# Second MoE, first product: product 6 joins products 1, 7 and 4 in one PSUM bank

## The chip, the cores and the metric

The kernel runs on one core of a Trainium2 chip. The metric is the device time of one execution in microseconds (us). The kernel before takes 1375.94 us, the median of 3 runs (1375.69 to 1376.54).

## The reference, cut to what matters

Three layers follow each other: pooled attention, a first MoE block with softplus, and a second MoE block with a router. The change lies in the first product of the second MoE block, `x @ w1[e]`, with the relu behind it:

```
def _moe2_ref(x, expert_emb, tau, w1, w2):
    N, D = x.shape                       # 4608, 512
    ...                                  # router: expert_idx, gate_w
    for e in range(E):
        mask = expert_idx == e
        h = np.maximum(x[mask] @ w1[e], 0.0)          # w1[e]: 512 x 1024
        out[mask] = gate_w[mask, None] * (h @ w2[e])
```

## The kernel before, in words

The second MoE block is computed for the expert that has most tokens over all 4608 tokens; other experts' tokens are left to a loop behind it, which has nothing to do in the run shown. The tokens come in 9 groups of 512 (`p` = 0 to 8), called pairs here, since each is two halves of 256 tokens. For every pair `mm3s(p, sg)` is called with `sg` 0 and 1, and each call makes two steps `j` of 128 hidden columns (with their partners 512 columns on). So there are 18 calls and 36 steps.

One step is a Strassen-like scheme with seven products in place of eight: two halves of `w1` rows, two of its columns, two halves of the tokens. A product (`prod`) is six matmuls of 128x128 by 128x256 into a PSUM bank: two chunks of 128 rows, and for each the three float32r products of high and low parts (`three`, lines 656 to 658). Products 1, 2 and 3 read the tokens (tile `b`), 4 to 7 read sums of them (tile `T`, made by `make_t` on GpSimd and `split_t` on ScalarE and VectorE). The results wanted are: 1+2 (hidden low, tokens low), 1+6+3+5 (low, high), 1+6+7+5 (high, high) and 1+6+7+4 (high, low). `put` makes two float32r parts of relu of such a result: ScalarE writes the high part (line 1025), VectorE the rest (line 1026).

TensorE's and SyncE's orders are those of the code. The orders of VectorE, ScalarE and GpSimd in this stage come from the framework's scheduler, so a new code order may reorder them. All engines work in order. `both` runs the two steps of a call, then three pieces of the second product (`mm4s`, nine matmuls of 128x512), then the last step's `end`, then the other 13 pieces. Where a bank is written again (`skip_group_check`), the first matmul of the product waits until the reading of the bank is done; with its weight load waits.

TensorE's order of products is, for the two steps of a call (the second with a prime): before 1, 6, 5, 2, 7, 1', 4, 3, 6', 5', 2', 7', three pieces, 4', 3'. The bank `b2` gathers products 6, 7 and 4, `b3` gathers 5 and 3, `b1` gathers 1 and 2. Four PSUM banks, with the tags `h` and `a` (two each), go round by the list `M_TAGS`.

Of the kernel before, what the change touches and what calls it, by code (L numbers as in the profile page):

```python
# [13 lines left out]
ALU = mybir.AluOpType  # L14
# [6 lines left out]
def tile_attention_moe_moe(  # L21
# [13 lines left out]
    nc = tc.nc  # L35
# [40 lines left out]
    def f32(ap):  # L76
        return ap.bitcast(F32)
# [5 lines left out]
    half = cp.tile([P, TPB], F32, name="half")  # L83
# [571 lines left out]
    def three(ps, lh, ll, rh, rl, first, last, more=False):  # L655
        nc.tensor.matmul(ps, ll, rh, start=first, stop=False, skip_group_check=more)  # L656
        nc.tensor.matmul(ps, lh, rl, start=False, stop=False, skip_group_check=more)  # L657
        nc.tensor.matmul(ps, lh, rh, start=False, stop=last, skip_group_check=more)  # L658
# [337 lines left out]
    def g_tile(k):  # L996
        pool = {"g": p2[0], "st": stp, "W": wp, "wo": wop}[HOMES[k]]
        kw = {"bufs": 3} if HOMES[k] == "g" else {}
        return pool.tile([P, 2, PT], F32R, tag=HOMES[k], name=f"g{k}", **kw)


    def mm3s(p, sg):
        x, t = b_t[p], t_t[p]
        direct = {1: 0, 2: 2, 3: 1}
        sums = {4: 1, 5: 0, 6: 2, 7: 3}

        def prod(bank, i, j, first):
            if i in direct:
                bh, bl = x[direct[i]][:, 0], x[direct[i]][:, 1]
            else:  # L1010
                bh, bl = t[:, 0, sums[i]], t[:, 1, sums[i]]
            ff = slice(j * P, (j + 1) * P)
            for c in range(2):
                w = a_t[i, c]
                three(bank, w[:, 0, ff], w[:, 1, ff], bh[:, c, :], bl[:, c, :], first and c == 0, c == 1, not first)

        def bank():
            tag = M_TAGS.pop(0)
            M_TAGS.append(tag)
            return (ps_h if tag == "h" else ps_a).tile([P, HT], F32, tag=tag, name="m")  # L1020


        def put(src, d, th):
            tt = slice(th * HT, (th + 1) * HT)
            nc.scalar.activation(d[:, 0, tt], src, AF.Relu)
            nc.vector.scalar_tensor_tensor(d[:, 1, tt], src, 0.0, f32(d)[:, 0, tt], ALU.max, ALU.subtract)

        def half(n):
            return p2[0].tile([P, HT], F32, tag=n, bufs=2, name=n)

        ends = []
        for j in (2 * sg, 2 * sg + 1):
            b1 = bank()
            prod(b1, 1, j, True)
            s1 = half("c1")
            nc.scalar.copy(s1, b1)
            if ends:
                ends.pop()()
            b2 = bank()
            prod(b2, 6, j, True)  # L1040
            s2 = half("c2")
            nc.vector.tensor_tensor(s2, b2, s1, ALU.add)
            b3 = bank()
            prod(b3, 5, j, True)
            prod(b1, 2, j, False)
            lo, hi = g_tile(2 * j), g_tile(2 * j + 1)
            gs_t[j], gs_t[j + 4] = lo, hi
            put(b1, lo, 0)
            prod(b2, 7, j, False)
            s3 = half("c3")  # L1050
            nc.vector.tensor_tensor(s3, b2, s1, ALU.add)
            nc.vector.tensor_tensor(s3, b3, s3, ALU.add)
            put(s3, hi, 1)

            def end(j=j, b2=b2, b3=b3, s1=s1, s2=s2, lo=lo, hi=hi):
                prod(b2, 4, j, False)
                nc.vector.tensor_tensor(s1, b2, s1, ALU.add)
                put(s1, hi, 0)
                prod(b3, 3, j, False)
                nc.vector.tensor_tensor(s2, b3, s2, ALU.add)  # L1060
                put(s2, lo, 1)

            ends.append(end)
        yield
        ends.pop()()

    M_TAGS = ["h", "h", "a", "a"]

    def mm4s(p, sg):
        if sg == 0 and p not in y_t:  # L1070
# [171 lines left out]
    with tc.block(schedule_with_timeline_sim=True), tc.manual_schedule(engines={mybir.EngineType.PE, mybir.EngineType.SP}):  # L1242
# [91 lines left out]

        load_b(1, (0, 1, 2))
        m3 = mm3s(0, 0)
        next(m3)
        run_mm2(*pend.pop(0))
# [3 lines left out]
        run(make_t(1))  # L1342
        fronts(WAIT + 1)
        both(mm3s(0, 1), mm4s(0, 0), WAIT2 + 3)
        for p in range(1, NPR):
            run(split_t(p))
            fronts(2)
            if p + 1 < NPR:
                load_b(p + 1)
                run(make_t(p + 1))  # L1350
            both(mm3s(p, 0), mm4s(p - 1, 1))
            fronts(1)
            both(mm3s(p, 1), mm4s(p, 0))
# [39 lines left out]
```

## Time and profile before

| | before |
|---|---|
| time, median of 3 runs | 1375.94 us |
| profiled execution: its own time | 1376.53 us |
| profiled execution: span of the trace | 1374.7 us |
| TensorE busy | 1350.0 us, 98% |
| VectorE busy | 763.5 us, 56% |
| ScalarE busy | 644.5 us, 47% |
| GpSimd busy | 281.4 us, 20% |
| share of TensorE in the chain that ended last | 83% |

The busy share of TensorE is near the whole span, so what matters in a stage is what TensorE waits for there. The second MoE block fills the stretch from about 974 us to the end.

### The profile page before, as it was taken

How to read it: one execution, taken by the hardware profiler on the slowest of the kernel's cores; microseconds unless marked ns; L12 is line 12 of the kernel's file. 1: busy time of each engine (PE TensorE's matmuls, PEld its weight loads, DVE VectorE, ACT ScalarE, POOL GpSimd, SP SyncE). 2: the span in 40 equal slices, each digit the busy share in tenths (PEclk: the TensorE clock that was granted, in tenths of full speed). 3: DMA queues.
4: the chain of work that ended last, by engine and by line, in shares of the span. 5: the costliest groups of instructions: out<-in, count | busy, mean ns of one | idle time of the engine just before them, and what ended most of it. 6: DMA issues, size and time to landing. Idle time of an engine off the chain costs nothing.

```text
span 1374.7 us, 18505 instructions
## 1 busy us (share of the span) xinstructions
PE 1350.0 (98%) x6998; PEld 1118.0 (81%) x6998; DVE 763.5 (56%) x1608; ACT 644.5 (47%) x1287; POOL 281.4 (20%) x268
## 2 busy tenths in 40 slices
PE   8999999999999999999999999999999999999998
PEld 7666678878888878888888888878878898998986
DVE  7997567566465466475564443353664544544432
ACT  5766455554465464564464454455532322222221
POOL 6500112121021020020020010073353022231100
PEclk9999999999999999999999999999999999999999
DMA  9742354353364363453442242563332212222000
GB/s 275 244 125 85 105 172 140 112 195 107 113 203 124 95 195 92 127 181 95 139 153 85 79 152 77 168 210 126 107 124 93 87 37 77 78 93 93 31 31 32
DMA packets 113564, 166.94 MB, mean 121 GB/s; under 512 B 42808, under 2 KB 69432, under 8 KB 113472
## 3 DMA queue, kind: packets, MB, share of 16 engines
q1 hardware_dynamic: 113472, 165.72, 38.2%
q8 instruction: 57, 0.93, 0.3%
q14 instruction: 35, 0.29, 0.1%
HBM read 128.99 MB, written 36.70 MB: 121 GB/s over the span
## 4 chain that ended last, share of the span: by engine, by line
PE 83%; DVE 8%; DMA 3%; POOL 2%; ACT 2%; issue 1%; SPq 1%; POOLq 0%; DVEq 0%; ACTq 0%
PE h L656 8%; PE h L658 8%; PE h L657 8%; PE acc L656 8%; PE acc L658 8%; PE acc L657 8%; PE y L656 5%; PE y L657 5%; PE y L658 5%; PE m L656 4%; PE m L658 4%; PE m L657 4%; PE pp L338 2%; PE acc L710 2%; PE lg L742 1%; DMA wos<-wo 1%
## 5 line engine op out<-in xcount | busy, mean ns | idle before, releaser
L656 PE MATMUL h<-x,wi 128*128 128x512 f32 x576 | 234.9, 408 | 1.2 <-DVE t L689 1.1
L658 PE MATMUL h<-x,wi 128*128 128x512 f32 x576 | 225.7, 392 | 0.0
L657 PE MATMUL h<-x,wi 128*128 128x512 f32 x576 | 225.0, 391 | 0.0
L672 ACT ACTIVATE t<-h 128x512 f32<-128x512 f32 x144 | 86.1, 598 | 229.5 <-PE h L658 222.7
L656 PE MATMUL acc<-g,ring 128*128 128x512 f32 x448 | 177.9, 397 | 0.1
L658 PE MATMUL acc<-g,ring 128*128 128x512 f32 x448 | 174.8, 390 | 0.0
L657 PE MATMUL acc<-g,ring 128*128 128x512 f32 x448 | 174.4, 389 | 0.0
L689 DVE SCALAR_TENSOR_TENSOR t<-h,t 128x512 f32<-128x512 f32 x128 | 87.9, 687 | 147.3 <-ACT t L676 146.1
L656 PEld LDWEIGHTS h<-x,wi 128*128 128x128 f32 x576 | 108.7, 189 | 24.4 <-DVE t L689 1.8
L658 PEld LDWEIGHTS h<-x,wi 128*128 128x128 f32 x576 | 108.4, 188 | 24.2
L657 PEld LDWEIGHTS h<-x,wi 128*128 128x128 f32 x576 | 108.8, 189 | 21.1 <-issue 1.0
L691 ACT CAST g<-t 128x512 fp32r<-128x512 f32 x128 | 79.6, 622 | 86.7 <-DVE t L689 86.6
L693 DVE TENSOR_TENSOR g<-t,g 128x512 fp32r<-128x512 f32 x128 | 92.0, 719 | 50.7 <-ACT g L691 50.6
L656 PE MATMUL y<-w,g 128*128 128x512 f32 x288 | 113.0, 392 | 0.0
L657 PE MATMUL y<-w,g 128*128 128x512 f32 x288 | 112.9, 392 | 0.0
L658 PE MATMUL y<-w,g 128*128 128x512 f32 x288 | 112.9, 392 | 0.0
L658 PEld LDWEIGHTS acc<-g,ring 128*128 128x128 f32 x448 | 84.1, 188 | 18.4
L656 PEld LDWEIGHTS acc<-g,ring 128*128 128x128 f32 x448 | 84.2, 188 | 16.2 <-issue 0.6
L657 PEld LDWEIGHTS acc<-g,ring 128*128 128x128 f32 x448 | 84.2, 188 | 15.8
L358 POOL TENSOR_TENSOR e<-e,sm 128x576 f32<-128x576 f32 x34 | 39.4, 1159 | 270.9 <-DVE sm L355 223.5
L676 ACT ACTIVATE t<-t 128x512 f32<-128x512 f32 x144 | 91.4, 635 | 2.9
L674 ACT ACTIVATE t<-t 128x512 f32<-128x512 f32 x144 | 91.5, 636 | 2.1
(228 smaller groups left out, 2713.9 us busy)
## 6 DMA issues: line engine op xcount, KB each, us to landing
ring<-wos SPq DMA_DIRECT2D x112, 512.0 KB, 3.7
x2s<-x SPq DMA_DIRECT2D x9, 2048.0 KB, 8.3
b<-x2s SPq DMA_DIRECT2D x27, 512.0 KB, 5.2
out_dram<-o SPq DMA_DIRECT2D x36, 256.0 KB, 2.1
st<-in_k_dram SPq DMA_DIRECT2D x16, 512.0 KB, 5.1
q<-in_q_dram SPq DMA_DIRECT2D x32, 256.0 KB, 4.3
st<-in_v_dram SPq DMA_DIRECT2D x16, 512.0 KB, 6.7
st<-in_moe_w_in_dram SPq DMA_DIRECT2D x16, 512.0 KB, 7.0
```

Of the source, the lines that this page charges most:

```text
L338: nc.tensor.matmul(pp[p0:p0 + n, i, :], qT[:, j, p0:p0 + n], kbd_t[b][:, j, :], start=True, stop=True)
L358: eng.tensor_tensor(e, e, sm1.unsqueeze(2).to_broadcast([P, H, SP]), ALU.mult)
L656: nc.tensor.matmul(ps, ll, rh, start=first, stop=False, skip_group_check=more)
L657: nc.tensor.matmul(ps, lh, rl, start=False, stop=False, skip_group_check=more)
L658: nc.tensor.matmul(ps, lh, rh, start=False, stop=last, skip_group_check=more)
L672: nc.scalar.activation(t, h, AF.Abs)
L674: nc.scalar.activation(t, t, AF.Exp, scale=-1.0)
L676: nc.scalar.activation(t, t, AF.Ln, bias=1.0)
L689: nc.vector.scalar_tensor_tensor(t, h, 0.0, t, ALU.max, ALU.add)
L691: nc.scalar.copy(g[:, 0, :], t)
L693: nc.vector.tensor_tensor(g[:, 1, :], t, f32(g)[:, 0, :], ALU.subtract)
L710: nc.tensor.matmul(accs[blk][d], wof[fc][:, dd], f32(g)[:, 0, :], start=first, stop=(fc == NFC - 1))
```

## The change

Bank `b1` now gathers products 1, 6, 7 and 4. ScalarE copies the partial sum out after product 1 (as before), after 1+6 (new line 1043) and after 1+6+7 (new line 1051). Product 2 goes to a bank of its own, and one VectorE addition joins it with the copy of product 1 (line 1048). The results 1+6+7+5 and 1+6+3+5 are additions of `b3` to the copies (lines 1053 and 1060), and 1+6+7+4 needs none: `put` reads it from the bank. The three additions of lines 1042, 1051 and 1057 of before are gone. TensorE's order becomes 1, 5, 6, 2, 7, 1', 4, 3, 5', 6', 2', 7', three pieces, 4', 3'; the number of matmuls stays. The list of bank tags follows.

```
             s1 = half("c1")
             nc.scalar.copy(s1, b1)
             if ends:
                 ends.pop()()
-            b2 = bank()
-            prod(b2, 6, j, True)
-            s2 = half("c2")
-            nc.vector.tensor_tensor(s2, b2, s1, ALU.add)
             b3 = bank()
             prod(b3, 5, j, True)
-            prod(b1, 2, j, False)
+            prod(b1, 6, j, False)
+            s2 = half("c2")
+            nc.scalar.copy(s2, b1)
+            b2 = bank()
+            prod(b2, 2, j, True)
             lo, hi = g_tile(2 * j), g_tile(2 * j + 1)
             gs_t[j], gs_t[j + 4] = lo, hi
-            put(b1, lo, 0)
-            prod(b2, 7, j, False)
+            nc.vector.tensor_tensor(s1, b2, s1, ALU.add)
+            prod(b1, 7, j, False)
             s3 = half("c3")
-            nc.vector.tensor_tensor(s3, b2, s1, ALU.add)
+            nc.scalar.copy(s3, b1)
+            put(s1, lo, 0)
             nc.vector.tensor_tensor(s3, b3, s3, ALU.add)
             put(s3, hi, 1)
 
-            def end(j=j, b2=b2, b3=b3, s1=s1, s2=s2, lo=lo, hi=hi):
-                prod(b2, 4, j, False)
-                nc.vector.tensor_tensor(s1, b2, s1, ALU.add)
-                put(s1, hi, 0)
+            def end(j=j, b1=b1, b3=b3, s2=s2, lo=lo, hi=hi):
+                prod(b1, 4, j, False)
+                put(b1, hi, 0)
                 prod(b3, 3, j, False)
                 nc.vector.tensor_tensor(s2, b3, s2, ALU.add)
                 put(s2, lo, 1)
...
-    M_TAGS = ["h", "h", "a", "a"]
+    M_TAGS = ["h", "h", "a", "a", "a", "h", "h", "h", "a", "a", "a", "h"]
```

The scheduler's orders move with it. On VectorE, for the first step of pair 5 (`g_10575` and `g_10576` are the low and high halves of the hidden tile, `c` the copies and sums in SBUF, `m` a bank), there stands before:

```order
L1042 TENSOR_TENSOR c_10560<-m,c_10551 128x256
L1026 SCALAR_TENSOR_TENSOR g_10575<-m,g_10575 128x256
L1051 TENSOR_TENSOR c_10585<-m,c_10551 128x256
L1052 TENSOR_TENSOR c_10585<-m,c_10585 128x256
L1057 TENSOR_TENSOR c_10551<-m,c_10551 128x256
L1026 SCALAR_TENSOR_TENSOR g_10576<-c_10585,g_10576 128x256
L1060 TENSOR_TENSOR c_10560<-m,c_10560 128x256
L1026 SCALAR_TENSOR_TENSOR g_10576<-c_10551,g_10576 128x256
```

and now:

```order
L1048 TENSOR_TENSOR c_10551<-m,c_10551 128x256
L1026 SCALAR_TENSOR_TENSOR g_10575<-c_10551,g_10575 128x256
L1053 TENSOR_TENSOR c_10584<-m,c_10584 128x256
L1026 SCALAR_TENSOR_TENSOR g_10576<-c_10584,g_10576 128x256
L1026 SCALAR_TENSOR_TENSOR g_10576<-m,g_10576 128x256
L1060 TENSOR_TENSOR c_10566<-m,c_10566 128x256
L1026 SCALAR_TENSOR_TENSOR g_10575<-c_10566,g_10575 128x256
```

The first line 1026 has moved from a bank (`m`) to two operands in SBUF (`c` and `g`), and stands ahead of the addition that frees bank `b3` (line 1053, before line 1052). On ScalarE the same step has before:

```order
L1036 COPY c_10551<-m 128x256
L1025 ACTIVATE g_10575<-m 128x256
L1036 COPY c_10597<-m 128x256
L1025 ACTIVATE g_10576<-c_10585 128x256
L1025 ACTIVATE g_10576<-c_10551 128x256
L1025 ACTIVATE g_10575<-c_10560 128x256
```

and now, with the next step's first two copies (`c_10598`, `c_10630`):

```order
L1036 COPY c_10551<-m 128x256
L1043 COPY c_10566<-m 128x256
L1025 ACTIVATE g_10575<-c_10551 128x256
L1051 COPY c_10584<-m 128x256
L1036 COPY c_10598<-m 128x256
L1025 ACTIVATE g_10576<-c_10584 128x256
L1025 ACTIVATE g_10576<-m 128x256
L1025 ACTIVATE g_10575<-c_10566 128x256
L1043 COPY c_10630<-m 128x256
```

The copy of 1+6+7 stands behind the relu of line 1025 that waits for the new addition, and the copy of 1'+6' behind three relus of the step before. In pair 1 the router's small operations on `n` and `z` lie between. VectorE has there now:

```order
L1048 TENSOR_TENSOR c_8906<-m,c_8906 128x256
L770 TENSOR_SCALAR n<-n,taut 128x4
L771 RECIPROCAL n<-n 128x4
L1026 SCALAR_TENSOR_TENSOR g_8930<-c_8906,g_8930 128x256
L775 TENSOR_TENSOR z<-z,n 128x32
L1053 TENSOR_TENSOR c_8939<-m,c_8939 128x256
```

where before only line 770 stood between the readings of the two banks:

```order
L1042 TENSOR_TENSOR c_8915<-m,c_8906 128x256
L1026 SCALAR_TENSOR_TENSOR g_8930<-m,g_8930 128x256
L1051 TENSOR_TENSOR c_8940<-m,c_8906 128x256
L770 TENSOR_SCALAR n<-n,taut 128x4
L1052 TENSOR_TENSOR c_8940<-m,c_8940 128x256
```

So the reading of `b3` has moved behind two more operations, lines 1026 and 775, that read SBUF alone. SyncE's order is the same.

## Rows read from the trace of the kernel before

**Rows 1.** Busy time by engine in the stage (us, instructions), granted clock, DMA share

```profile
974.40:1349.00 374.60, 371.07 (x2336) 333.82 (x2335) 185.44 (x437) 109.70 (x261) 93.39 (x73) 1.00 0.22 74
```

**Rows 2.** What TensorE waited for in the stage: us, times, longest

```profile
PE m L656 <- DVE c L1042: 2.7, 3, 1.6
PE m L656 <- DVE c L1052: 0.8, 1, 0.8
```

**Rows 3.** Timeline, TensorE: one long wait; last of 18 short ones (start, us)

```profile
1153.93 0.39 PE L656 MATMUL m<-T,a 128*128 128x256 f32 x1 [0.88 <-DVE c L1042]
...
1340.38 0.38 PE L656 MATMUL m<-T,a 128*128 128x256 f32 x1
```

**Rows 4.** Groups by line and shape in the stage: busy us, mean ns

```profile
L1026 DVE SCALAR_TENSOR_TENSOR g<-c,g 128x256 fp32r<-128x256 f32 x107 | 57.1, 540 | 10.0 <-ACT g L1025 9.5
L1026 DVE SCALAR_TENSOR_TENSOR g<-m,g 128x256 fp32r<-128x256 f32 x36 | 15.2, 423 | 37.1 <-ACT g L1025 37.1
L1036 ACT COPY c<-m 128x256 f32<-128x256 f32 x36 | 13.4, 373 | 83.1 <-PE m L658 83.1
```

**Rows 5.** Timeline of pair 3, first call (PEld is the weight load)

```profile
1103.11 0.28 PE L658 MATMUL m<-b,a 128*128 128x256 f32 x1
...
1103.49 0.37 ACT L1036 COPY c<-m 128x256 f32<-128x256 f32 x1 [7.67 <-PE m L658]
...
1103.83 0.19 PEld L656 LDWEIGHTS m<-T,a 128*128 128x128 f32 x1
...
1106.33 0.41 DVE L1051 TENSOR_TENSOR c<-m,c 128x256 f32<-128x256 f32 x1
...
1106.68 0.28 PE L658 MATMUL m<-b,a 128*128 128x256 f32 x1
...
1106.80 0.19 PEld L656 LDWEIGHTS m<-T,a 128*128 128x128 f32 x1
...
1107.00 0.38 ACT L1036 COPY c<-m 128x256 f32<-128x256 f32 x1 [1.05 <-PE m L658]
...
1107.27 0.42 ACT L1025 ACTIVATE g<-c 128x256 fp32r<-128x256 f32 x1
...
1107.81 0.42 DVE L1057 TENSOR_TENSOR c<-m,c 128x256 f32<-128x256 f32 x1 [0.61 <-PE m L658]
...
1108.26 0.42 ACT L1025 ACTIVATE g<-c 128x256 fp32r<-128x256 f32 x1 [0.57 <-DVE c L1057]
```

**Rows 6.** Timeline of pair 4: VectorE's line 1026 and GpSimd beside it

```profile
1150.54 1.29 POOL L976 TENSOR_TENSOR bf<-bf 128x512 f32<-128x512 f32 x1
...
1150.60 1.51 DVE L1026 SCALAR_TENSOR_TENSOR g<-c,g 128x256 fp32r<-128x256 f32 x1
```

**Rows 7.** Timeline of pairs 2 and 5: first matmul, GpSimd's last sum

```profile
1060.28 0.28 PE L656 MATMUL m<-b,a 128*128 128x256 f32 x1
...
1063.73 1.29 POOL L978 TENSOR_TENSOR bf<-bf 128x512 f32<-128x512 f32 x1
...
1188.33 0.28 PE L656 MATMUL m<-b,a 128*128 128x256 f32 x1
...
1192.23 1.29 POOL L978 TENSOR_TENSOR bf<-bf 128x512 f32<-128x512 f32 x1
```

**Rows 8.** Timeline of pair 1, first call: first matmul, router's line 770, GpSimd

```profile
1014.92 0.39 PE L656 MATMUL m<-b,a 128*128 128x256 f32 x1
...
1019.47 1.24 DVE L770 TENSOR_SCALAR n<-n,taut 128x4 f32<-128x4 f32 x1 [0.22 <-POOL n L768]
...
1020.65 1.28 POOL L974 TENSOR_TENSOR bf<-bf 128x512 f32<-128x512 f32 x1
...
1022.01 1.29 POOL L976 TENSOR_TENSOR bf<-bf 128x512 f32<-128x512 f32 x1
```

**Rows 9.** Timeline of pair 0, second call: first matmul, first copy

```profile
990.82 0.28 PE L656 MATMUL m<-b,a 128*128 128x256 f32 x1
...
992.27 0.40 ACT L1036 COPY c<-m 128x256 f32<-128x256 f32 x1
```

## Prediction

> **What bounds the kernel now.** I read the table of stretches first: in the stage of the change TensorE is busy for 371.07 of 374.60 us at full granted clock, while VectorE is busy for 185.44 and ScalarE for 109.70 [rows 1]. So nothing is gained by taking work off VectorE as such. Only two things can move the end: what TensorE waits for now, and what it will wait for instead. The list of waits gives the first: four waits of 3.5 us in all, three for the addition of line 1042 and one for line 1052 [rows 2]. A wait costs more than the idle time shown. In the long one of [rows 3] the matmul is 0.39 us long in place of 0.28, and the matmul ahead of it would have been overlapped by 0.16 (0.28 less a spacing of 0.12). So each wait costs its idle time plus about 0.26, and the four cost 3.5 + 4 x 0.26 = **4.6 us**. The timeline shows 18 short ones besides, one in each call, that the list of waits doesn't show: a matmul of 0.38 us with no idle time ahead of it, at product 4 of the first step [rows 3]. In pair 3 its weight load starts at 1106.80, where one spacing behind the last matmul's own load it would have started at about 1106.69, just as that matmul (1106.68) starts [rows 5]. That is 0.1 us each, **1.8 us** for 18. All that the change can win in this stage is therefore 6.4 us.
>
> **What is removed.** Three additions a step go, 36 x 3 of some 0.42 us on VectorE. This is off the path, except where TensorE waited for them: the 6.4 us above. I take all of that off, and put back below what TensorE waits for in the new order.
>
> **The copies on ScalarE.** 72 copies are added, 0.373 us each [rows 4], and they lie in 265 us of idle time of ScalarE. But TensorE now waits for copies. Product 6 follows product 1 into the same bank with one product (5) between, product 7 follows 6 with one product (2) between, and product 4 follows 7 with one (1') between. Before, the copy and the first addition had two products of cover. What one product covers is seen in pair 3 [rows 5]: the last matmul of product 1 starts at 1103.11 and the weights of the product after next load at 1103.83, so 0.72 us. The copy starts at 1103.49, 0.38 behind that matmul's start, and ends at 1103.86; the other copy starts 0.32 behind (1107.00 against 1106.68). From the end of a reading to the weight load is 0.06 (the addition ends at 1106.74, the load starts at 1106.80). So a copy needs 0.32 to 0.38, plus 0.37, plus 0.06: 0.75 to 0.81 us against 0.72. Each single cover is missed by 0.03 to 0.09.
>
> The Trainium skill, "ScalarE: Activation LUTs", section "What ACT_TABLE_LOAD costs", gives an ACTIVATE with immediate operands 186 ns plus 0.833 ns per element, 399 ns here; the trace has 373 for the copy, so the measurement decides. By the page's figure each of the single covers would be missed by 0.03 more, some 2 us in all.
>
> Product 4 has more. The copy of 1+6+7 stands behind the relu that waits for the new addition. By the durations of [rows 5], counted from the start of product 2's last matmul: addition from 0.35 to 0.77, relu from 0.80 (0.03 behind an addition, as 1108.26 behind 1108.23), the next ScalarE operation 0.27 to 0.30 later, at 1.07 to 1.10. Product 7 alone would allow it at 0.71 + 0.35 = 1.06. So the relu holds it by some 0.03, and product 4 is late by 0.05 to 0.12, about what it is late now. In a call the single covers are: 6, 7 and 4 of the first step and 7' of the second (6' has three products of cover, and 4' has the three pieces). I take 0.06 + 0.06 + 0.09 + 0.06 = 0.27 a call, **4.9 us** for 18; the bounds are 3 x 0.03 + 0.05 = 0.14 and 3 x 0.09 + 0.12 = 0.39, so 2.5 to 7.0 us.
>
> **The subtraction that now reads SBUF alone.** Line 1026 takes 423 ns with a bank as its operand and 540 in the mean with two operands in SBUF [rows 4]. The excess is not spread evenly: beside a running GpSimd sum one takes 1.51 us, and ends 0.28 behind that sum's end (1152.11 against 1151.83) [rows 6]. Before, no such operation stood ahead of the readings that TensorE waits for in the first step. Now one stands ahead of line 1053, which frees bank `b3` for product 3. It becomes due about 4.1 us behind the first matmul of a pair: 2.9 for the last matmul of product 2 (four products of 0.715, less a spacing, plus 0.15 of the new waits), then 0.35 + 0.42 for the addition and 0.03 + 0.42 for the relu. GpSimd's last sum for the next pair runs then. In pair 2 it ends at 1065.02, 4.74 behind the first matmul; in pair 5 at 1193.52, 5.19 behind [rows 7]; pairs 3, 6 and 7 lie between. Line 1053 then ends 0.28 + 0.34 + 0.06 later, and product 3's weights load 0.05 behind: 0.7 us behind GpSimd's end, against a time without waits of 5.1 (seven products, less 0.11, plus 0.2 of new waits). Pair 2 loses 0.35, pair 5 0.8. For five pairs I take **2.5 us**; it is 0 if the subtraction isn't held.
>
> The Trainium skill, "SBUF — State Buffer", section "SBUF: two separate sides", says that a VectorE operation with two SBUF inputs and a GpSimd operation share a port pair as an exclusive lock, held for the whole instruction. The trace agrees: 1.51 us beside GpSimd, 0.42 from a bank. By the rule the sum gets these 2.5 us, without it none.
>
> **Pair 1.** The router's operations lie between here. Line 770 runs from 1019.47 to 1020.71; the subtraction behind it meets GpSimd's sum that ends at 1021.93, and line 775 behind that the next, which ends at 1023.30 [rows 8]. Line 1053 can't end before about 1023.75, and product 3 would load at 1014.92 + 5.2 = 1020.1. That is 3.7 us late, where line 1052 cost 1.1 before. The three relus ahead of the second step's copy of 1'+6' are late with it, and cost product 7' some 0.6 more, in place of 1.9 now. Together **4.3 us**, bounds 2.5 to 5.5.
>
> **The rest.** In pair 0's second call the first copy ends at 992.67 behind squares and casts; product 6, due at 990.82 + 1.32 = 992.14, loads at 992.73 [rows 9]: **0.5 us** beyond the 0.06. The router's logits then take the bank of product 4' of that call, which is read by a relu and a subtraction with one product as cover: 0.35 + 0.39 + 0.03 + 0.42 + 0.06 = 1.25 less 0.72, 0.5 us. Pairs 0 and 4 have GpSimd sums all through the first step, and the subtraction may meet the gap between two of them or not: 0 to 1.1 each. I take **1.0 us** for all of this, 0.5 to 2.5.
>
> **Sum.** Added: 4.9 + 2.5 + 4.3 + 0.5 + 1.0 = 13.2 us; taken off: 6.4. Net +6.8 against the profiled execution's own 1376.53 us (span 1374.7, 1.8 around it); that run lies 0.6 above the median of 1375.94, so the median becomes 1382.7. I say **1382.5 us**. SyncE's order and the number of matmuls don't move; the last pair has no GpSimd sums, and its last results have the 13 pieces and 16 more as cover, so the end of the kernel moves only with TensorE.
>
> **Rivals.** (1) *Faster.* The copies are done in time, so that TensorE waits for none, and with VectorE relieved the long waits vanish. The whole 6.4 goes: 1369.5. It decides at 0.72 us: reading, copy and signal would have to fit into one product. For it speaks that they miss it by 0.03 only, at best; against it that both copies in [rows 5] miss it, and that the long waits depend on GpSimd and the router, which stay. With the short waits at their lower bound and no holding, it would be 1375.9 - 6.4 + 2.5 = 1372. Together 0.08. (2) *No change.* The subtraction finds gaps between GpSimd's sums, or the sums run a little earlier; pair 1 costs what it cost (3.0): 4.9 + 3.0 + 0.5 less 6.4 is +2.0, and -0.4 with the short waits at 2.5: 1375.5 to 1378. Chance 0.2. (3) *Slower still.* ScalarE's queue couples with VectorE: if the copy of 1+6+7 in each call is held by a whole relu more (0.3 us), 18 x 0.3 = 5.4 come on top, 1388. Its point is the addition of line 1048: it has to be 0.3 late in every call. Only pairs 1 and 3, with router work on VectorE, speak for it. Chance 0.1. (4) The forecast, 1379 to 1386, has 0.62.
>
> **Numbers.** What a measurement of this kernel can tell from no change is 0.2%, 2.75 us. Slower by more than that (above 1378.7) has 0.62 + 0.1 = 0.72, within it 0.2, faster 0.08. The range from 1376.0 to 1386.5 leaves out rival 1, the lower edge of rival 2 and rival 3.
>
> **What would show it.** In the changed profile: TensorE's waits for ScalarE's lines 1043 and 1051, or matmuls of 0.3 to 0.4 us at the first matmuls of products 6, 7, 4 and 7' in every call; waits for line 1053 at product 3 in pairs 2, 3, 5, 6 and 7 of 0.3 to 0.8 us, each behind a line 1026 of over 1 us; one near 3.7 us in pair 1. No wait for VectorE in pairs 2 to 7 would make the second term wrong, and no long matmuls at products 6 and 7 the first. A wait list of less than 5 us in all would make the sign wrong.

## The result and the profile after

The changed kernel takes 1384.86 us, the median of 5 runs (1382.96 to 1386.14), beside 1376.25 (1375.69 to 1377.96, 5 runs) for the kernel before on the same chip. The ratio is 1.0059, 95% interval 1.0044 to 1.0074: slower, by more than the 0.2% that a measurement can tell.

The page's line of busy times, and then the table of stretches for the same span of the program as [rows 1] (us of the stretch, then busy us and instructions of TensorE, its weight loads, VectorE, ScalarE and GpSimd, the granted clock, the DMA share, GB/s):

```profile
PE 1357.6 (98%) x6998; PEld 1124.2 (81%) x6998; DVE 731.4 (53%) x1536; ACT 667.4 (48%) x1359; POOL 280.4 (20%) x268
```

```profile
974.40:1358.30 383.90, 379.13 (x2347) 340.57 (x2347) 153.08 (x365) 134.53 (x336) 93.07 (x73) 1.00 0.22 73
```

VectorE has lost 32 us of work in the stage against [rows 1] (185.44 to 153.08), and ScalarE has gained 25. Neither bounds anything. What counts is what TensorE waits for; the list of waits now has (engine, line and what was waited for; us in total, times, longest):

```profile
PE m L656 <- DVE c L1053: 3.9, 2, 3.5
PE m L656 <- ACT c L1036: 0.3, 1, 0.3
PE lg L742 <- DVE g L1026: 0.2, 1, 0.2
```

The three waits for line 1042 of [rows 2] have gone. The one for line 1052 (now line 1053, product 3 of pair 1) has grown from 0.8 to 3.5 us, and one of 0.5 in pair 7 has come beside it. The list leaves the short ones out, so I use one more measure from here on, the *lost time*: from each matmul's start I take the start of the one before and the ordinary spacing (0.118 us behind a matmul of 256 columns, 0.2285 behind one of 512), and add up over the stage what is left where it is over 0.03. It is 7.0 us in the kernel before and 13.7 in the changed one. The stage itself, from its first matmul to the last of the program, has grown from 393.2 us (974.73 to 1367.97) to 399.8 (977.40 to 1377.16), by 6.5.

The two profiled executions lie 9.6 us apart (1386.14 and 1376.53). Of the other 3.1, 2.7 lie ahead of the stage, which starts that much later. Some 1.6 of them come between 200 and 220 us, where this execution had the granted clock at 0.89 over 15 us (the 1.2 GHz level for a part of them) and a second one of the same kernel (the repeat below) did not; most of the rest come in the first 75 us. In the repeat the stage starts at 973.4, earlier than in the kernel before, so this part is not the change's; why the clock fell there (in e10_all_third too, near 206 us) stays open. First the changed kernel's row for that stretch, then the repeat's:

```profile
200.00:215.00 15.00, 13.53 (x65) 11.03 (x64) 12.06 (x25) 6.15 (x15) 2.17 (x2) 0.89 0.44 122
```

```profile
200.00:215.00 15.00, 13.53 (x73) 11.10 (x73) 11.23 (x26) 7.96 (x17) 2.40 (x2) 1.00 0.33 105
```

In the same time there are 65 matmuls in one and 73 in the other.

**The short waits.** Pair 3, first call, timeline (start, duration, engine, line). The rows are: last matmul of product 6, the copy of 1+6, last of product 2, first of product 7, the new addition, the relu behind it, the copy of 1+6+7, last of product 1', first of product 4.

```profile
1111.44 0.28 PE L658 MATMUL m<-T,a 128*128 128x256 f32 x1
...
1111.82 0.37 ACT L1043 COPY c<-m 128x256 f32<-128x256 f32 x1 [1.12 <-PE m L658]
...
1112.15 0.28 PE L658 MATMUL m<-b,a 128*128 128x256 f32 x1
1112.27 0.35 PE L656 MATMUL m<-T,a 128*128 128x256 f32 x1
...
1112.54 0.43 DVE L1048 TENSOR_TENSOR c<-m,c 128x256 f32<-128x256 f32 x1 [8.85 <-PE m L658]
...
1113.00 0.42 ACT L1025 ACTIVATE g<-c 128x256 fp32r<-128x256 f32 x1 [0.81 <-DVE c L1048]
...
1113.33 0.35 ACT L1051 COPY c<-m 128x256 f32<-128x256 f32 x1
...
1113.65 0.28 PE L658 MATMUL m<-b,a 128*128 128x256 f32 x1
1113.77 0.35 PE L656 MATMUL m<-T,a 128*128 128x256 f32 x1
```

The copy begins 0.38 behind the last matmul's start and ends at 1112.19, while the cover, product 2, is through at 1112.27. The matmul of 0.35 in place of 0.28 is all that shows; the next one starts 0.07 late. The same is there at product 4, whose copy stands behind the relu.

**The subtraction beside GpSimd.** First pair 7, where GpSimd's sum (POOL) holds it: the sum, line 1026, the addition that frees `b3`, the first matmul of product 3. Then pair 5, where it begins 0.12 ahead of one sum's recorded end (1197.95 + 1.30 = 1199.25), before the next has started.

```profile
1284.25 1.30 POOL L978 TENSOR_TENSOR bf<-bf 128x512 f32<-128x512 f32 x1
...
1284.47 1.36 DVE L1026 SCALAR_TENSOR_TENSOR g<-c,g 128x256 fp32r<-128x256 f32 x1 [0.48 <-ACT g L1025]
...
1285.75 0.41 DVE L1053 TENSOR_TENSOR c<-m,c 128x256 f32<-128x256 f32 x1
...
1286.22 0.39 PE L656 MATMUL m<-b,a 128*128 128x256 f32 x1 [0.50 <-DVE c L1053]
```

```profile
1197.95 1.30 POOL L976 TENSOR_TENSOR bf<-bf 128x512 f32<-128x512 f32 x1
...
1199.13 0.43 DVE L1026 SCALAR_TENSOR_TENSOR g<-c,g 128x256 fp32r<-128x256 f32 x1 [0.48 <-ACT g L1025]
...
1199.33 1.38 POOL L978 TENSOR_TENSOR bf<-bf 128x512 f32<-128x512 f32 x1
...
1199.48 0.42 DVE L1053 TENSOR_TENSOR c<-m,c 128x256 f32<-128x256 f32 x1
```

It ends 0.28 behind GpSimd's end in pair 7 (1285.83 against 1285.55), as in [rows 6], and costs product 3 0.76 of lost time; in pair 5 it takes 0.43 and costs nothing. It is held in pairs 2, 3 and 6 too, for a shorter time: it takes 0.78, 0.91 and 0.78 us, again ends 0.28 to 0.29 behind the sum's end, and product 3 loses 0.2 to 0.3. Pair 2:

```profile
1069.90 1.29 POOL L978 TENSOR_TENSOR bf<-bf 128x512 f32<-128x512 f32 x1
...
1070.70 0.78 DVE L1026 SCALAR_TENSOR_TENSOR g<-c,g 128x256 fp32r<-128x256 f32 x1 [0.48 <-ACT g L1025]
```

The second calls of pairs 1 to 8 are a comparison within the same execution: the copies are the same and the subtraction stands ahead of the addition too, but GpSimd has no sum running; the subtraction takes 0.42 to 0.43 each time, and product 3 loses nothing.

**Pair 1.** The router's line 770, GpSimd's sums, the subtraction, line 775, the addition, and TensorE's first three matmuls of product 3:

```profile
1023.45 1.25 DVE L770 TENSOR_SCALAR n<-n,taut 128x4 f32<-128x4 f32 x1 [0.91 <-POOL n L768]
...
1024.82 1.35 DVE L1026 SCALAR_TENSOR_TENSOR g<-c,g 128x256 fp32r<-128x256 f32 x1
1025.96 1.32 POOL L976 TENSOR_TENSOR bf<-bf 128x512 f32<-128x512 f32 x1
1026.09 1.25 DVE L775 TENSOR_TENSOR z<-z,n 128x32 f32<-128x32 f32 x1
1027.26 0.41 DVE L1053 TENSOR_TENSOR c<-m,c 128x256 f32<-128x256 f32 x1
...
1027.72 0.58 PE L656 MATMUL m<-b,a 128*128 128x256 f32 x1 [3.45 <-DVE c L1053]
...
1028.10 0.41 PE L657 MATMUL m<-b,a 128*128 128x256 f32 x1
...
1028.32 0.41 PE L658 MATMUL m<-b,a 128*128 128x256 f32 x1
```

```profile
1028.00:1031.00 3.00, 3.00 (x16) 3.00 (x17) 2.96 (x14) 1.03 (x4) 0.79 (x2) 0.53 0.00 0
1031.00:1035.00 4.00, 4.00 (x27) 3.61 (x26) 2.22 (x6) 1.48 (x4) 0.00 (x0) 1.00 0.00 0
```

The chain is the one foreseen. What follows the wait was not: the granted clock is 0.53 in the mean of 3 us (near the 1.2 GHz level), and matmuls are 0.21 apart in place of 0.12.

### The profile page after: what moved, and what is told of

It reads as the page before. It is cut to its first block, busy times and chain, and to the rows that moved or that the text cites. A ratio compares the mean times of both kernels' runs of the same rounds, so it can differ in the third digit from the quotient of the medians.

```text
span 1384.0 us, 18527 instructions
## 1 busy us (share of the span) xinstructions
PE 1357.6 (98%) x6998; PEld 1124.2 (81%) x6998; DVE 731.4 (53%) x1536; ACT 667.4 (48%) x1359; POOL 280.4 (20%) x268
## 4 chain that ended last, share of the span: by engine, by line
PE 82%; DVE 7%; DMA 4%; ACT 2%; POOL 2%; issue 1%; SPq 1%; POOLq 0%; DVEq 0%; ACTq 0%
PE h L656 8%; PE h L658 8%; PE h L657 8%; PE acc L656 8%; PE acc L658 7%; PE acc L657 7%; PE m L656 5%; PE y L657 5%; PE y L656 5%; PE y L658 5%; PE m L657 4%; PE m L658 4%; PE acc L710 2%; PE pp L338 2%; PE lg L742 1%; DMA wos<-wo 1%
```

## The experiments

Three cures were made, each for one term. *Cover*: pieces of the second product (three matmuls of 512 columns, 0.69 us) are put ahead of the products that follow with one product's cover. *Order*: the addition of line 1053 is held ahead of the subtraction with two SBUF operands. *Route*: the router's line 770 in pair 1 is held in the order of the code. The theory is that only TensorE's waits count, and that the change loses what the three cures address; the rival is that something else in the new order (ScalarE's load, or banks that come free later) makes it slow.

### e1_cover: pieces of the second product as cover

```
             if ends:
+                piece()
                 ends.pop()()
             b3 = bank()
             prod(b3, 5, j, True)
+            if j == 2 * sg:
+                piece()
             prod(b1, 6, j, False)
...
             nc.vector.tensor_tensor(s1, b2, s1, ALU.add)
+            piece()
             prod(b1, 7, j, False)
...
-            for _ in range(3):
+            for _ in range(2):
                 next(m4)
```

Here `piece` is `next(m4)` with the generator of the call's second product.

> The changed kernel with one piece of the second product (three matmuls, 0.69 us) put as cover ahead of products 6, 7 and 4 of the first step and of 7' of the second, and two in place of three ahead of 4'. Theory (each copy misses one product of cover, 0.28 us a call): the long matmuls at products 6, 7, 4 and 7' go in 17 calls (pair 0's first call has no pieces), 4.7 us; product 3 comes 2 us later, so its waits behind line 1026 go too, 1.4 us in pairs 2 to 7 and 2 to 3 of pair 1's 5: 1375 to 1377 us in all. Rival (the loss is pair 1's wait and the clock behind it, the short stretches cost nothing that the end sees): no more than 3 us, 1381 to 1383 us.

Measured: 1378.63 us (10 runs) beside 1376.36, ratio 1.0020 (1.0010 to 1.0029). Lost time 8.3. The short waits are gone in all calls but the first, and so are those at product 3 in pairs 2 to 7. But pair 1 still loses 7 us, in another place. The waits, then ScalarE and TensorE there, and the granted clock behind it:

```profile
PE m L656 <- ACT c L1059: 3.2, 1, 3.2
PE m L656 <- DVE c L1061: 0.8, 1, 0.8
```

```profile
1022.76 1.32 DVE L785 TENSOR_SCALAR eq<-z 128x32 f32<-128x32 f32 x1
...
1024.11 0.23 ACT L795 ACTIVATE z<-z 128x32 f32<-128x32 f32 x1 [1.82 <-DVE eq L785]
...
1024.24 0.35 ACT L1059 COPY c<-m 128x256 f32<-128x256 f32 x1
...
1024.65 0.58 PE L656 MATMUL m<-T,a 128*128 128x256 f32 x1 [3.16 <-ACT c L1059]
```

```profile
1026.00:1031.00 5.00, 4.16 (x20) 3.86 (x20) 3.59 (x10) 1.10 (x3) 0.74 (x1) 0.50 0.00 0
```

The scheduler has put a router operation of ScalarE (line 795) ahead of the copy of 1+6+7 (line 1059 here), and that waits for a VectorE operation (line 785) of 1.32 us beside GpSimd's sums, which takes 0.17 to 0.18 in the other eight blocks of tokens. So the cover takes off what it was made for. The time fits neither the theory's 1375 to 1377 us nor the rival's 1381 to 1383: it came out above the theory because pair 1 did not shrink.

### e2_order and e3_route: the addition first, then the router too

```
-            put(s1, lo, 0)
-            nc.vector.tensor_tensor(s3, b3, s3, ALU.add)
+            nc.scalar.activation(lo[:, 0, 0:HT], s1, AF.Relu)
+            tc.keep_in_program_order(nc.vector.tensor_tensor(s3, b3, s3, ALU.add))
+            tc.keep_in_program_order(
+                nc.vector.scalar_tensor_tensor(lo[:, 1, 0:HT], s1, 0.0, f32(lo)[:, 0, 0:HT], ALU.max, ALU.subtract)
+            )
```

and, in e3_route only, beside it:

```
-        nc.vector.tensor_scalar(n, n, 1e-6, taut, ALU.add, ALU.mult)
+        ins = nc.vector.tensor_scalar(n, n, 1e-6, taut, ALU.add, ALU.mult)
+        if blk == NB - 1:
+            tc.keep_in_program_order(ins)
```

> The changed kernel with VectorE's addition of line 1053 held ahead of the subtraction that reads SBUF alone. Theory (the subtraction, held by GpSimd, makes product 3 wait): the waits of product 3 in pairs 2 to 7 go, 1.4 us, and pair 1's shrinks by the 1.2 to 1.3 us of the subtraction, to some 2.3, with less or no slow clock behind it: 2.5 to 4 us less than the changed kernel. The short waits, 0.28 us a call, stay. Rival (the waits come from the copy of 1+6+7, not from the subtraction): product 3 waits as before, same time as the changed kernel.

> As the run with the order held, and the router's line 770 of the last block held behind the first product's operations of pair 1. Theory: pair 1 has no wait for VectorE left and no slow clock, so 3.6 + 1.3 us of it go beside the 1.4 of the other pairs: 1378 to 1380 us, with only the 0.28 us a call and pair 0's 1.5 left. Rival (GpSimd's sums hold VectorE's later operations in pair 1 as well): half of that, 1381 to 1382 us.

Measured: e2_order 1381.33 us (4 runs), ratio 1.0044 (1.0027 to 1.0060), lost time 11.6; e3_route 1378.85 (10 runs), ratio 1.0014 (1.0004 to 1.0023), lost time 9.2; both beside 1376.36. In e2_order the waits at product 3 in pairs 2 to 7 are all gone, and the one in pair 1 is shorter; the waits and the clock around pair 1:

```profile
PE m L656 <- DVE c L1053: 1.5, 1, 1.5
PE m L656 <- DVE g L1026: 1.1, 2, 0.8
```

```profile
1023.00:1030.00 7.00, 5.25 (x35) 4.67 (x36) 6.84 (x21) 2.37 (x7) 3.19 (x4) 1.00 0.00 0
```

Behind a wait of 1.5 us the granted clock stays at 1.00. A new wait comes, of 0.8 us: product 2' takes the bank of product 4, which the held subtractions now read later. In e3_route the wait for the addition in pair 1 is gone as well. What is left is the new wait at product 2' (1.4 us in pairs 0 and 1), the short ones, 0.28 us in each call, unchanged, and some 3 us at single products, most of them in pair 0 or at product 7'. The waits at product 3 went with the copies as they were, so the rival of e2_order falls.

### e4_all and e8_all_again: the three cures together

> The pieces as cover, the order held and the router's line 770 held, together. Theory: TensorE waits for nothing in this stage but 1 to 2 us in pair 0, so the 7 us that it waits in the kernel before are won as well: 1370 to 1372 us. Rival (the pieces taken from the tail leave the sums of the next pair or the second product's operands late): waits at products 5, 6 or at the pieces, 1373 to 1377 us.

> The changed kernel with all cures again, beside the kernel before with the same cures on the same chip: 2 us of waits in the stage, 3 to 5 us below the kernel before, and within 1 us of the kernel before with its cures if the waits are all that counts.

Measured: 1373.11 us (10 runs) beside 1376.36, ratio 0.9976 (0.9966 to 0.9986); again 1371.19 (5 runs) beside 1377.15, ratio 0.9961 (0.9946 to 0.9976). Lost time 2.1 and 2.2. So the three cures account for all but 2 of the 13.7 us. The first median lies above the theory's 1370 to 1372 and at the lower edge of the rival's range, the second within the theory's; the rival falls by its other mark, since what is left lies in pair 0 and at the router's matmuls, and products 5, 6 and the pieces wait for nothing in the other pairs. The second stands 6.0 us below the kernel before, more than the 3 to 5 expected. The subtraction is still held in this kernel, as in this row of pair 3, but nobody waits behind it:

```profile
1107.29 1.39 DVE L1065 SCALAR_TENSOR_TENSOR g<-c,g 128x256 fp32r<-128x256 f32 x1
```

### e5_again: the changed kernel once more

> The changed kernel itself once more, to part what the stage costs from what the granted clock does elsewhere. Theory (the change costs what TensorE waits for in the second block, 6.7 us more than before by the two traces, and up to 2 us of slow clock that follows pair 1's wait; the rest of the first difference of 8.6 us is a stretch of slow clock near 210 us that has nothing to do with the change): 6 to 8 us above the kernel before, and waits of 13 to 14 us in the stage. Rival (the change slows the earlier stages too): 8.5 us or more, with the stage's start at 977 us again and its waits unchanged.

Measured: 1383.16 us (4 runs) beside 1377.15, ratio 1.0050 (1.0032 to 1.0068). Lost time 14.2, with the same pattern: 0.28 a call, and 3.8 at product 3 in pair 1 with the lower clock behind it. The stage starts at 973.4 us, so the rival, that earlier stages are slower, falls. Only the pairs in which the subtraction is held differ: pairs 3 and 4 lose 0.8 and 0.6, pairs 5 and 7 nothing. Whether it meets a gap between two sums of GpSimd changes from one execution to the next.

### e6_before_sbuf: the kernel before with this subtraction alone

```
-            put(b1, lo, 0)
+            s4 = half("c3")
+            nc.scalar.copy(s4, b1)
+            put(s4, lo, 0)
```

> The kernel before with one thing of the change alone: ScalarE copies the sum 1+2 out, and the low half's relu and subtraction read the copy, so that the subtraction has two operands in SBUF ahead of the addition that frees bank b3. Theory (GpSimd holds that subtraction): waits at product 3 of 0.3 to 0.8 us in most of the pairs 2, 3, 5, 6 and 7, and more than before in pairs 1 and 4, 2 to 4 us in all: 1378 to 1380 us. Rival (the subtraction's place is harmless, the loss is in the copies' cover): no wait at product 3 in pairs 2 to 7 and the same time as before, 1376.

Measured: 1379.94 us (10 runs) beside 1377.15, ratio 1.0019 (1.0009 to 1.0028). Lost time 10.8 in place of 7.0. The waits, and pair 4:

```profile
PE m L656 <- DVE c L1054: 5.0, 9, 2.2
PE m L656 <- DVE c L1042: 1.6, 1, 1.6
```

```profile
1151.85 1.29 POOL L974 TENSOR_TENSOR bf<-bf 128x512 f32<-128x512 f32 x1
1152.14 1.29 DVE L1026 SCALAR_TENSOR_TENSOR g<-c,g 128x256 fp32r<-128x256 f32 x1
...
1153.35 0.41 DVE L1054 TENSOR_TENSOR c<-m,c 128x256 f32<-128x256 f32 x1
...
1153.82 0.39 PE L656 MATMUL m<-b,a 128*128 128x256 f32 x1 [0.57 <-DVE c L1054]
```

With nothing of the change but the two SBUF operands and the copy that they need, a wait for the addition behind product 5 (line 1054 here, 1052 before) comes in the first call of every pair but the last, and once more in pair 0's second call: 7.5 us of lost time at product 3 in place of 1.1, of which 2.6 in the first calls of pairs 2, 3, 5, 6 and 7. In the second calls, where the same copy and order meet no sum of GpSimd, product 3 loses nothing but 0.15 in pair 3. So it is the subtraction beside GpSimd, and not the added copy, that costs the time: this shows the term by itself.

### e7_before_free, e9_before_free2 and e10_all_third: the same cures for the kernel before

The kernel before was given a piece ahead of product 4 (one less behind the call's steps) and the route; e7_before_free holds line 1042's addition in the order of the code, e9_before_free2 line 1052's instead. e10_all_third is the changed kernel with the three cures again. The two expectations for the kernel before name more pieces than the edits have: both put one piece ahead of product 4, and none ahead of 6, 7 or 7'. The edit of e9_before_free2, without the route:

```
             if ends:
+                piece()
                 ends.pop()()
             b2 = bank()
...
-            nc.vector.tensor_tensor(s3, b3, s3, ALU.add)
+            tc.keep_in_program_order(nc.vector.tensor_tensor(s3, b3, s3, ALU.add))
```

> The kernel before with the same cures: a piece ahead of product 4 and of 7' (and of 6 and 7), and the router's line 770 held behind pair 1's first products. Theory (TensorE's time in this stage is its waits and nothing else, whoever makes the sums): nearly the same as the changed kernel with its cures, 1370 to 1373 us, within 1 us of it. Rival (five VectorE additions load VectorE so that it is late elsewhere, and three cost less once TensorE is covered): 2 us or more slower than the changed kernel with its cures.

> The kernel before with the three cures that apply to it: two pieces of the second product ahead of product 4, the two-operand-from-PSUM addition behind product 5 held in program order, and the router's mask held likewise. Theory (only the waits of TensorE count, five additions or three do not matter once they are covered): extra time of TensorE in the stage 1.5 to 4, median within 1.5 us of the changed kernel with all cures, 1370 to 1374. Rival (the new order is worth something of its own, because five additions keep VectorE from answering in time): short waits stay at several products and it is 2 us or more slower than the changed kernel with all cures, 1375 or above.

> The changed kernel with all cures, once more beside the kernel before with its cures, on the same chip: 1371 to 1374, extra time of TensorE in the stage 2 to 2.5. Theory: the other stands within 1.5 us of it. Rival: the other stands 2 us or more above it.

Measured: e7_before_free 1387.48 us (4 runs) beside 1377.15, ratio 1.0086 (1.0068 to 1.0104). It says nothing of the two schemes. The held addition fell behind another operation that came late (line 748, which waits 3.4 us for ScalarE):

```profile
998.85 0.69 DVE L748 TENSOR_TENSOR sh<-ss,sh 128x512 fp32r<-128x512 f32 x1 [3.44 <-ACT sh L747]
999.46 0.42 DVE L1049 TENSOR_TENSOR c<-m,c 128x256 f32<-128x256 f32 x1
...
999.93 0.58 PE L656 MATMUL m<-T,a 128*128 128x256 f32 x1 [5.39 <-DVE c L1049]
```

and in pair 3's second call behind the small VectorE operations that make the list of other experts' blocks (lines 1112 to 1137), 4.2 us. So e8_all_again's comparison with it on the same chip tells nothing either.

e9_before_free2: 1372.93 us (10 runs), ratio 0.9974 (0.9965 to 0.9984); e10_all_third: 1372.45 (7 runs), ratio 0.9967 (0.9956 to 0.9979), both beside 1376.71 on the same chip. Lost time 2.4 and 2.1. The stage's rows, first of the kernel before with cures, then of the changed one with cures:

```profile
974.40:1349.00 374.60, 373.74 (x2353) 336.34 (x2352) 190.62 (x438) 110.91 (x263) 94.45 (x73) 1.00 0.23 74
```

```profile
974.40:1349.00 374.60, 373.97 (x2354) 336.20 (x2353) 160.29 (x366) 136.95 (x334) 93.88 (x73) 1.00 0.23 74
```

VectorE is busy for 30 us more in the one, and TensorE is busy to 0.2 us alike; from the stage's first matmul to the last it is 389.0 and 388.8 us. The medians lie 0.5 us apart, within the noise, and the rival's 2 us are not there. So with the waits covered no gain or loss of the change is seen, and what it cost was its waits. By the ratios of all four runs both beat the kernel before by 0.24 to 0.39%.

## Why the prediction was right

The forecast was slower by 6.6 us, with 13.2 us added and 6.4 taken off (the sum's 6.8, rounded down to 1382.5). The lost time gives the same account, by terms:

| term | forecast | measured |
|---|---|---|
| taken off: long and short waits of before | 6.4 | 6.7 |
| short waits for ScalarE's copies, 18 calls | 4.9 | 4.8 |
| subtraction held, pairs 2, 3, 5, 6, 7 | 2.5 | 1.4 (0.2, 0.3, 0, 0.2, 0.8) |
| pair 1 | 4.3 | 5.1 (3.7 wait, 1.4 clock) |
| first copy of pair 0's second call | 0.5 | 0.6 |
| the rest | 1.0 | 1.4 |

A further 0.3 us, in which other work shows in both kernels, stands on both sides (13.4 + 0.3 and 6.7 + 0.3). Before rounding, the added terms come to 13.4, and 6.7 net.

**What is removed.** In lost time the four long waits of before measure 4.6 us, as taken, the 18 short ones 1.9, and two small ones beside them 0.2. What stands at the same products in the changed kernel is counted in the other rows. That three additions a step leave VectorE shows no worth of its own: e9_before_free2 and e10_all_third agree to 0.5 us.

**The copies.** Each of products 6, 7, 4 and 7' loses 0.06 to 0.08, within the bounds of 0.03 and 0.09, and product 4 at the low end of its 0.05 to 0.12. Only the cover takes this away (e1_cover, e4_all); order and route leave it at 0.28 a call.

**The subtraction.** The mechanism is right: e6_before_sbuf has it alone, and e2_order takes the waits away by moving the operation alone. It comes due 4.10 us behind a pair's first matmul, as forecast (4.1). The term was mis-sized, since it took the subtraction to be held in all five pairs: pair 5, priced at 0.8, met a gap between two sums and lost nothing, and in pairs 2 and 6 the sum ended 4.6 us behind the first matmul in place of 4.74 or later. In the profiled execution the gap was met in pairs 4 and 5, in the repeat in pairs 5 and 7. The Trainium skill, "SBUF — State Buffer", section "SBUF: two separate sides", has the lock held for a whole instruction. The rows agree but for some 0.15 us: held, the subtraction ends 0.28 behind the sum's recorded end, less than its plain 0.43, and in pair 5 it began 0.12 ahead of one.

**Pair 1.** The wait at product 3 is 3.7 us as forecast. The 0.6 for product 7' did not come (0.07). Something else did, which the prediction did not have: the clock's fall behind the wait, 1.4 us. It is there in the repeat too; e2_order, with the wait at 1.5, doesn't show it.

**The rest.** The router's logits lose 0.4, where 0.5 was taken. The others are the first call's product 6 (0.4), product 3 of pair 0's second call (0.3) and product 7' of pair 7 (0.3).

So three terms are right in size, and two errors, -1.1 in the subtraction and +0.8 in pair 1, nearly cancel. That the net lost time came out within 0.1 us of the sum's 6.8 is luck to that extent. The measured medians are 8.6 and, in the repeat, 6.0 above those of before, while the lost time says 6.7. The spread between the runs of one kernel is 2 to 6 us; the one piece of it that I followed is the clock at 200 to 215 us, which is not the change's.

Of the rivals, no change needed the subtraction free and pair 1 as it was; the coupling that was to make it slower still is not seen, since product 4 loses no more than the other products. That the scheme could be faster is true only with the cover that it lacks, and then not for the reason given there.

## What to carry to other kernels

Where one engine bounds a stage, work taken off another engine is worth nothing; count for each bank that is written again what stands between its last matmul and its next one, and compare reading, copy and signal with that cover to a hundredth of a microsecond, times the number of calls. An operand moved from PSUM to SBUF can cost more than the operation itself, if GpSimd runs beside it and a bank's release stands behind it in the queue. And the cheap remedy is often independent work already in the program, placed in the gap; but hold the order of a scheduler's operations one at a time, since a held operation can fall behind one that is late (e7_before_free).

## What the runs showed of the hardware

- The granted clock of TensorE fell behind long waits inside a dense stream: to 0.53 in the mean of 3 us, near the 1.2 GHz level, behind one of 3.45 us of idle time, and to 0.50 behind one of 3.16 us with another of 0.84 after it (e1_cover). It fell to the same level behind idle times of 4.03 and 5.39 us (e7_before_free). It stayed at 1.00 behind 1.5 us (e2_order), 1.64 (the kernel before) and 2.2 (e6_before_sbuf). I had priced a long wait by its length alone.
- A subtraction on VectorE with two SBUF operands that begins 0.12 us ahead of the recorded end of a GpSimd sum, 0.20 ahead of the next one's start, takes its plain 0.43 us, while the GpSimd sum that starts beside it takes 1.38 in place of 1.30 (pair 5). Held, it ends 0.28 behind GpSimd's end, the same in [rows 6] and in pairs 2, 3 and 7 of the changed kernel, however long it was held (0.78 to 1.51 us in all). With one operand in a PSUM bank it took 0.41 to 0.43 us in all 36 cases of the kernel before, beside GpSimd's sums or not.
